# A late table, a shared opening and an earlier split: rearranging the start and the first group change of a gated linear attention and expert kernel

## The chip, the cores and the metric

The kernel runs on one core of a Trainium2 chip. The metric is the time of one execution on the device in microseconds (us). A core has five engines that each work through their own queue of instructions in order: TensorE (PE in the profile, PEld where it loads weights), VectorE (DVE), ScalarE (ACT), GpSimd (POOL) and SyncE (SP), which here only issues transfers. A queue's own instructions, such as the issue of a transfer, carry a q behind the engine's name (SPq, ACTq).

## The reference

Two blocks follow each other. The first is a gated linear recurrence over 768 time steps for 4 batches and 8 heads of 48 columns; the second is four experts of two layers each, weighted by normalised probabilities.

```python
for t in range(S):                      # B 4, H 8, S 768, D 48
    state = alpha[:, :, t, :, None] * state + einsum('bhd,bhe->bhde', k[:, :, t], v[:, :, t])
    y[:, :, t] = einsum('bhd,bhde->bhe', q[:, :, t], state)
x = y.transpose(0, 2, 1, 3).reshape(B * S, H * D)          # 3072 x 384
p = domain_probs / (domain_probs.sum(-1, keepdims=True) + 1e-09)
for e in range(4):                                          # w1 384 x 1024, w2 1024 x 384
    out += p[:, e:e + 1] * (np.maximum(x @ w1[e], 0.0) @ w2[e])
```

## The kernel before

**Units and groups.** A unit is 128 time steps of one batch; there are 24. A unit's attention yields 128 rows of x, transposed. Units are collected into groups: group 0 has two, groups 1 to 5 have four each, the last has two. A group is what the experts work on at a time.

**The attention of one unit** (`attention(u)`) is a generator. It loads nothing itself but asks for the raw inputs of a later unit as its own come free (`load(after, ...)`). It turns alpha, k and q on PE (`turned`, L270), copies alpha's and k's result out of PSUM on ScalarE (tile AT, L281; tile KT, L286), and multiplies q's by AT on VectorE (tile QT, L293). The terms of a row with itself are a product and a sum on VectorE (L289, L290, tile `dot`). Then come seven levels, each with twice the block width of the last: two ScalarE copies of a half of QT into a block tile (`copy_q`, L312), a product of QT with the decay (`next_q`, L319, and the decay's own product, L321), a ScalarE copy of a half of KT into the next KT tile (L330) and a VectorE product for the other half (L331, `next_k`). PE multiplies the blocks (`products`, L338; `far`, L393 for the last level), and VectorE puts the scores in their places under a mask (`take`, L348) in the tile `near`, which starts from the terms of a row with itself (L364). At the end ScalarE copies `far` (L406) and `near` (L410, twice, once for each half) into the tile `lat`, PE multiplies that with v (`yps`, L432), and ScalarE puts the result into the group's x (L448).

**The experts.** `up(gi, e, fc)` computes one of eight chunks of 128 hidden columns for a whole group; `down(gi, e, slots, between)` multiplies them with the second layer's weights for a unit and adds the sums up on VectorE or ScalarE (`add_up`). In group 0 the first layer works on plain float32 (L538). From group 1 on, x and the weights are split into parts with fewer bits each (`split_x`, `split_piece`), and L546 multiplies the parts: part 1 and 0 into the tile `one`, part 2 into `two`. Step 0 of `split_x` is three ScalarE copies (L502) that make part 0; each of the steps 1 to 3 makes the parts 1 and 2 of a third of x on VectorE (L252, L253). Split weights are written to DRAM from GpSimd's queue (`kept<-w`, L233) and read again by the later groups (L196).

**Order.** The program writes out the order of instructions itself; each engine takes them in that order. At the start, unit 0 runs alone with dummy matmuls (`fill`, L749) in between, so that PE stays busy; unit 1 follows behind, at first interleaved with it. From then on, `advance` adds up estimated costs of the expert work, and steps a unit's generator when its due time has come. Each step of `down` is one product of a unit with a chunk; `between` holds pieces of work to be put ahead of a given step. That is how the next group's x is split during the last second layer of the group before (expert 3). For group 0 that layer is called twice, once for each of its two units, with eight steps each.

**Loads.** The loads of the units and of the weights are issued from SP in the order of the program: `load(0, "akqv")`, `load(1, "akqv")`, and then the four pieces of the first expert's first layer (`load_piece(0, i)`, L214 and L215). The identity, the masks and the probabilities (`p_all`, 48 KB in runs of four floats) come from ScalarE's queue. `norm_probs` normalises the probabilities on VectorE after unit 0's attention (L257 to L261), and they are used when sums are added up.

Of the kernel before, what the change touches and what calls it, by code (L numbers as in the profile page):

```python
# [10 lines left out]
F32 = mybir.dt.float32  # L11
# [5 lines left out]
AX = mybir.AxisListType  # L17
# [3 lines left out]
def kernel(  # L21
# [37 lines left out]
    nc = tc.nc  # L59

    B, H, S, D = q.shape
    E, DM, F = moe_w1.shape
    P = 128
# [7 lines left out]
    NT = B * P  # L71
# [11 lines left out]
    n = np.arange(QUAD)[None, :]  # L83
# [7 lines left out]
    work = ctx.enter_context(tc.tile_pool(name="work", bufs=2))  # L91
# [7 lines left out]
    p_all = const.tile([P, NBLK, E], F32, name="p_all")  # L99
# [3 lines left out]
    near = const.tile([P, H, HALF], F32, name="near")  # L103
    lat = const.tile([P, H, P], F32, name="lat")
# [26 lines left out]
    def raw(u, nm):  # L131
        return values[u % 2] if nm == "v" else apart[nm] if u == 1 else early[nm]
# [27 lines left out]
    def load(u, names):  # L160
        if u >= len(units):
            return
        cb, b = units[u]
        for nm in names:
            src = srcs[nm][b, :, cb * P:(cb + 1) * P, :].rearrange("h s d -> s h d")
            if nm != "v":
                nc.sync.dma_start(out=raw(u, nm)[:, :, :D], in_=src)
                continue

            pairs = raw(u, nm).rearrange("p (a i) d -> p a i d", i=2)  # L170
            src = src.rearrange("p (a i) d -> p a i d", i=2)
            nc.sync.dma_start(out=pairs[:, :, 0, :D], in_=src[:, :, 0])
            nc.sync.dma_start(out=pairs[:, :, 1, :TAIL], in_=src[:, :, 1, QUAD:])
            nc.sync.dma_start(out=pairs[:, :, 1, TAIL:D], in_=src[:, :, 1, :QUAD])
# [13 lines left out]
    def load_piece(l, i, beside=False):  # L188
        if i >= E * NQ * LAST:
            return  # L190
        gi, k = divmod(i, E * NQ)
        e, c = divmod(k, NQ)
        if gi > l:
            w = wt[l][i] = wts.tile([P, 3, KC * QF], F32R, name=f"w{l + 1}",
                                    bufs=AHEAD if l == 0 else NQ)
            nc.sync.dma_start(out=w.bitcast(F32), in_=kept[l][k])  # L196
            return
        if l == 1 and not beside:
            return
        if l == 0:  # L200

            if gi > 0 or e == 0:
                shared[c] = wts.tile([P, 3, KC * QF], F32R, name="w2", bufs=NQ)
            w = shared[c][:, 2 - e % 2 if gi == 0 else 2].bitcast(F32)
        else:

            place = (hidden[c][:, 0] if not split2(gi, e, c) else hidden[c + NQ // 2][:, 1])
            w = place.rearrange("p f n -> p (f n)")[:, :KC * QF].bitcast(F32)
        wt[l][i] = w
        if l == 0:  # L210
            heads = moe_w1[e].rearrange("(h d) f -> h d f", d=D)[:, :, c * QF:(c + 1) * QF]
            w = w.rearrange("p (c f) -> p c f", f=QF)
            for part in range(2):
                nc.sync.dma_start(out=w[:, part], in_=heads[part * H // 2:(part + 1) * H // 2, :QUAD])  # L214
            nc.sync.dma_start(out=w[:, 2], in_=heads[:, QUAD:])  # L215
        else:
            nc.sync.dma_start(
                out=w.rearrange("p (c d) -> p c d", d=DM),
                in_=moe_w2[e].rearrange("(c p) d -> p c d", p=P)[:, c * FPQ:(c + 1) * FPQ])
# [44 lines left out]
    def halves(t, m):  # L264
        return t.rearrange("p a (b two r) -> p a b two r", two=2, r=m)

    def turned(src):
        tp = ps.tile([P, NP, P], F32, name="tp", tag="w")
        for p in range(NP):
            nc.tensor.transpose(tp[:, p, :], src(p), ident)  # L270
        return tp

    def attention(u):
        cb, b = units[u]
        ra, rk, rq, rv = (raw(u, nm) for nm in ("a", "k", "q", "v"))
# [6 lines left out]
        after = u + 2 if u == 0 else u + 1 if u > 1 else len(units)  # L282
# [1 line left out]
        yield  # L284
        KT = keys()
        nc.scalar.copy(out=KT, in_=turned(pair(rk)))  # L286
        own = work.tile([P, NT], F32, name="t")[:, :H * D].rearrange("p (h d) -> p h d", d=D)
        dot = work.tile([P, H], F32, name="dot")
        nc.vector.tensor_mul(own, rq[:, :, :D], rk[:, :, :D])  # L289
        nc.vector.reduce_sum(out=dot, in_=own, axis=AX.X)  # L290
        load(after, "k")
        yield
        nc.vector.tensor_mul(QT, turned(pair(rq)), AT)  # L293
        load(after, "q")
        yield

# [27 lines left out]
        def next_k(li):  # L324
            m = LEVELS[li]
            old = new = halves(KTs[li], m)
            if li + 1 < len(LEVELS):
                KTs.append(keys())
                new = halves(KTs[-1], m)
                nc.scalar.copy(out=new[:, :, :, 1, :], in_=old[:, :, :, 1, :])  # L330
            nc.vector.tensor_mul(new[:, :, :, 0, :], old[:, :, :, 0, :],  # L331
                                 spread(halved(decs[li])[:, :, :, 1], m))

# [70 lines left out]
        for s in range(2):  # L404
            rows = slice(HALF * s, HALF * (s + 1))
            nc.scalar.copy(out=parts[:HALF, :, s, :, HALF:], in_=far[rows])  # L406
        yield
        for s in range(2):
            rows = slice(HALF * s, HALF * (s + 1))
            nc.scalar.copy(out=lat[rows, :, rows], in_=near[rows])  # L410
        KT = KTs[-1]
        yield

# [49 lines left out]
        if cb < NCB - 1:  # L463
# [5 lines left out]
            for i in range(2):  # L469
                rows = slice(HD * i, HD * (i + 1))  # L470
                old, add = st[rows, :, i, :], sps[rows, :, i, :]
# [251 lines left out]
    with tc.manual_schedule():  # L723
        nc.scalar.dma_start(out=ident_all, in_=nc.inline_tensor(ident_np, name="ident_c").ap())
        nc.scalar.dma_start(out=masks, in_=nc.inline_tensor(mask_np, name="masks_c").ap())
        nc.scalar.dma_start(out=p_all, in_=moe_domain_probs.rearrange("(n p) e -> p n e", p=P))
        nc.gpsimd.memset(sts[B - 1], 0.0)
        for nm in "akq":
            for r in (early[nm], apart[nm]):
                nc.gpsimd.memset(r[:, :, D:], 0.0)  # L730
        nc.gpsimd.memset(lat[HALF:, :, :HALF], 0.0)
        for t in values + blocks:
            nc.gpsimd.memset(t, 0.0)
        for t in sts[:-1]:
            nc.gpsimd.memset(t, 0.0)

        load(0, "akqv")
        load(1, "akqv")
        for i in range(NQ):
            load_piece(0, i)  # L740

        idle = ps.tile([P, P], F32, name="idle", tag="g", bufs=4)
        zeros = sts[B - 1].rearrange("p a i d -> p (a i d)")[:, :P]

        def fill(n):
            for _ in range(n):
                nc.tensor.matmul(idle, lhsT=zeros, rhs=zeros, start=True, stop=True)  # L749

        runs = [attention(u) for u in range(len(groups[0]))]
        fill(8)
        for u, n in ((0, 3), (0, 6), (0, 4), (0, 5), (0, 5), (0, 4), (0, 3), (1, 0), (0, 0), (0, 2),
                     (0, 2), (1, 2), (0, 2), (1, 0), (0, 0), (0, 4), (0, 4), (0, 0)):
            next(runs[u])
            fill(n)
        norm_probs()

        span = cost(0, 0, 0) * FCH / 2 + cost(1, 0, 0)
        waiting.extend((span * (k + 1) / 15, u, runs[u])  # L760
                       for k, u in enumerate([1, 1, 1, 0, 1, 0, *[1] * 8]))
        for fc in range(FCH):
            up(0, 0, fc, slice(0, 1))
            advance(cost(0, 0, 0) / 2)
        down(0, 0, [0], deque())
        while waiting:
            next(waiting.popleft()[2], None)
        clock = 0.0
        waiting.extend((1.0 + k, 1, runs[1]) for k in range(2))
        waiting.extend(deal())  # L770

        for (gi, e), after in zip(tasks, [*tasks[1:], (None, None)]):
            rest = gi == e == 0
            for fc in range(FCH):
                up(gi, e, fc, slice(1, len(groups[0])) if rest else None)
                advance(cost(0, gi, e) / (2 if rest else 1))
            each = len(groups[gi]) if split2(gi, e) else 1
            turns = [range(k, k + each) for k in range(rest, len(groups[gi]), each)]
            for k, slots in enumerate(turns):

                between = deque()
                if after[1] == 0:
                    for step, at in enumerate((0.0, 0.6, 0.7, 0.78)):
                        at = at * len(turns) - k
                        if 0 <= at < 1:
                            between.append((at, lambda step=step: split_x(after[0], step)))
                down(gi, e, slots, between)
        while stores:
            stores.popleft()()
# [28 lines left out]
```

## The time and the profile before

| What | Value |
|---|---|
| Time, median of 3 runs | 1064.21 us (1062.67 to 1064.66) |
| Span of the profiled execution | 1062.8 us |
| Mean granted clock of PE | 0.998 |
| PE busy | 1041.9 us, 98% |
| VectorE busy | 781.6 us, 74% |
| ScalarE busy | 569.0 us, 54% |
| GpSimd busy | 32.9 us, 3% |
| First matmul of the first layer starts | 26.22 us |
| First matmul of group 1's first layer starts | 165.66 us |

Busy time is the time in which an engine worked on an instruction, and a share of it is an average over all stages: it tells which engine can be the limit, not where. A line of the timeline gives the start in microseconds from the span's start, the duration, the engine, the source line, the operation, the tiles written and read, and how many like instructions follow each other; in brackets stands how long the engine was idle before it, and what it then waited for. A line of the waits gives the engine and the line that waited, what it waited for, the total in microseconds, how often, and the longest.

### The profile page before, as it was taken

Reading aid. Unit: us, or ns where it says so; the run is one execution under the profiler, and the core shown is the slowest. Engines: PE = TensorE matmul, PEld = TensorE weight load, DVE = VectorE, ACT = ScalarE, POOL = GpSimd, SP = SyncE. Lnnn points to the kernel's source line nnn. Section 1 sums busy time; section 2 is a strip of 40 time slices with the busy share of each in tenths; the row PEclk is TensorE's granted clock in tenths of the full one; section 3 lists DMA queues with packets and bytes.
Section 4 is the critical chain, followed back from the end, with each engine's and each line's share of the span. In section 5 each row is a group of like instructions: output and inputs, shape, how many; then the busy total and the mean of one; then the engine's idle time right before and its main releaser. Section 6 shows DMA issues by size and latency. Waiting matters only on the chain.

```text
span 1062.8 us, 21599 instructions
## 1 busy us (share of the span) xinstructions
PE 1041.9 (98%) x8508; PEld 906.2 (85%) x8508; DVE 781.6 (74%) x1619; ACT 569.0 (54%) x1202; POOL 32.9 (3%) x71
## 2 busy tenths in 40 slices
PE   8899999999999999999999999999999999999998
PEld 7777776687788898898898998988989889898988
DVE  5488777677779877778877877986877875666565
ACT  5687875665756555536546435555464443323232
POOL 2010010000001000000000000000000000000000
PEclk9999999999999999999999999999999999999999
DMA  8596799797977957758669559586594454444531
GB/s 124 157 325 202 245 318 352 272 339 241 307 256 271 376 180 276 279 165 315 249 187 364 201 190 339 172 307 231 167 373 174 194 208 170 187 179 178 197 160 45
DMA packets 158838, 251.66 MB, mean 237 GB/s; under 512 B 120113, under 2 KB 135345, under 8 KB 136209
## 3 DMA queue, kind: packets, MB, share of 16 engines
q1 hardware_dynamic: 149600, 208.82, 57.3%
q0 software_dynamic: 5760, 41.29, 9.7%
q8 instruction: 67, 1.10, 0.4%
q10 hardware_dynamic: 3376, 0.17, 0.3%
q14 instruction: 35, 0.28, 0.1%
HBM read 207.79 MB, written 42.47 MB: 235 GB/s over the span
## 4 chain that ended last, share of the span: by engine, by line
PE 85%; ACT 5%; DVE 5%; DMA 2%; issue 2%; SPq 1%; ACTq 0%; DVEq 0%
PE ops L639 36%; PE one L546 23%; PE two L546 11%; PE sc L338 6%; PE yps L432 3%; PE tp L270 3%; ACT qb L312 2%; PE one L538 1%; PE sps L467 1%; PE far L393 1%; DMA hT<-in_moe_w_dram 1%; DVE w L230 1%; ACT KT L330 1%; DMA rq<-in_q_dram 1%; SPq L214 1%
## 5 line engine op out<-in xcount | busy, mean ns | idle before, releaser
L639 PE MATMUL ops<-w,hT 128*128 128x384 f32 x1872 | 347.4, 340 | 0.2 <-DVE hT L592 0.2
L639 PEld LDWEIGHTS ops<-w,hT 128*128 128x128 f32 x1872 | 325.4, 188 | 4.7 <-ACT t L557 0.6
L546 PE MATMUL one<-xT,w 128*128 128x512 f32 x960 | 254.4, 400 | 2.7 <-DVE xT L252 2.3
L546 PEld LDWEIGHTS one<-xT,w 128*128 128x128 f32 x960 | 176.3, 189 | 42.2 <-DVE xT L252 4.0
L557 ACT ACTIVATE t<-one 128x512 f32<-128x512 f32 (+1 forms) x192 | 107.2, 558 | 180.7 <-PE one L546 175.3
L312 ACT COPY qb<-QT 64x256 f32<-64x256 f32 x336 | 136.6, 407 | 71.2 <-DVE QT L293 42.7
L586 DVE SCALAR_TENSOR_TENSOR hT<-t,hT 128x512 fp32r<-128x512 f32 (+1 forms) x172 | 110.5, 643 | 68.3 <-ACT hT L584 65.8
L559 DVE TENSOR_TENSOR t<-t,two 128x512 f32<-128x512 f32 (+1 forms) x172 | 109.5, 636 | 58.0 <-ACT t L557 29.3
L584 ACT ACTIVATE hT<-t 128x512 fp32r<-128x512 f32 (+1 forms) x172 | 101.8, 592 | 86.4 <-DVE t L559 85.3
L546 PE MATMUL two<-xT,w 128*128 128x512 f32 x480 | 136.9, 394 | 0.0
L546 PEld LDWEIGHTS two<-xT,w 128*128 128x128 f32 x480 | 90.6, 189 | 20.2 <-DVE acc L668 0.2
L639 PE MATMUL ops<-hT 128*128 128x384 f32 x288 | 100.9, 491 | 0.3 <-DMA hT<-in_moe_w_dram 0.3
L592 DVE SCALAR_TENSOR_TENSOR hT<-hT 128x512 fp32r<-128x512 f32 (+1 forms) x172 | 101.0, 634 | 0.0
L348 DVE COPY_PREDICATED near<-masks,sc 128x256 f32<-128x256 uint8 x144 | 76.9, 534 | 19.2 <-PE sc L338 16.3
L319 DVE TENSOR_TENSOR QT<-QT,dec 128x256 f32<-128x256 f32 x144 | 60.8, 423 | 36.0 <-ACT qb L312 35.3
L338 PEld LDWEIGHTS sc<-qb,KT 128*64 128x64 f32 x2304 | 72.7, 138 | 9.3 <-issue 4.7
L338 PE MATMUL sc<-qb,KT 128*64 128x64 f32 x2304 | 77.2, 223 | 2.6 <-ACT qb L312 2.6
L639 PEld LDWEIGHTS ops<-hT 128*128 128x128 f32 x288 | 52.1, 190 | 29.6 <-DMA hT<-in_moe_w_dram 0.9
L668 DVE SCALAR_TENSOR_TENSOR acc<-ops,p_all,acc 128x384 f32<-128x384 f32 x82 | 49.9, 615 | 30.4 <-PE ops L639 29.2
L330 ACT COPY KT<-KT 128x256 f32<-128x256 f32 x144 | 60.0, 417 | 3.1
L331 DVE TENSOR_TENSOR KT<-KT,dec 128x256 f32<-128x256 f32 x144 | 60.2, 418 | 0.0
L538 PE MATMUL one<-xT,w 128*128 128x256 f32 (+1 forms) x240 | 46.2, 340 | 0.6 <-ACT xT L448 0.6
(88 smaller groups left out, 934.2 us busy)
## 6 DMA issues: line engine op xcount, KB each, us to landing
w<-kept SPq DMA_DIRECT2D x144, 1152.0 KB
kept<-w POOLq DMA_DIRECT2D x32, 1152.0 KB, 7.9
hT<-in_moe_w_dram SPq DMA_DIRECT2D x32, 384.0 KB
w<-in_moe_w_dram SPq DMA_DIRECT2D x48, 128.0 KB
ra<-in_alpha_dram SPq DMA_DIRECT2D x23, 192.0 KB
rk<-in_k_dram SPq DMA_DIRECT2D x23, 192.0 KB
rq<-in_q_dram SPq DMA_DIRECT2D x23, 192.0 KB
out_dram<-acc POOLq DMA_DIRECT2D x18, 192.0 KB, 7.9
```

What stands on the lines that cost most here:

```text
L312: nc.scalar.copy(out=qb[rows, :, i, :].rearrange("p a (b r) -> p a b r", r=m), in_=qv[rows])
L319: nc.vector.tensor_mul(qv, qv, spread(dv[:, :, :, 0], m))
L330: nc.scalar.copy(out=new[:, :, :, 1, :], in_=old[:, :, :, 1, :])
L338: nc.tensor.matmul(out[HALF * s:HALF * (s + 1), 2 * p:2 * p + 2, :], lhsT=KTs[li][:, p, HALF * s:HALF * (s + 1)], rhs=qbs[li][:, p, :, QUA ...
L348: nc.vector.copy_predicated(near.rearrange("p a (b two r) -> p a b two r", two=2, r=m)[:, :, :, 1, :], mk.unsqueeze(1).broadcast_to([P, H, ...
L546: nc.tensor.matmul(out, lhsT=w[:, part, kc], rhs=x_part(gi, part, kc), start=(part == terms[0] and kc == 0), stop=(part == terms[-1] and k ...
L557: nc.scalar.activation(out=t, in_=one, func=ACT.Copy, scale=FINE)
L559: nc.vector.tensor_add(t, t, two)
L584: nc.scalar.activation(out=top, in_=x, func=ACT.Relu, scale=TRIM)
L586: nc.vector.scalar_tensor_tensor(out=low, in0=x, scalar=0.0, in1=top.bitcast(F32), op0=ALU.max, op1=ALU.subtract)
L592: nc.vector.scalar_tensor_tensor(out=dif, in0=top.bitcast(F32), scalar=1 / 4096.0, in1=low.bitcast(F32), op0=ALU.mult, op1=ALU.subtract)
L639: nc.tensor.matmul(sums[at], lhsT=h, rhs=w, start=(n == begins[at]), stop=(n == ends[at]))
```

## The change

The change has three parts.

The load of the probabilities goes from ScalarE's queue, where it was issued among the first inputs, to SP's queue behind the inputs of the first two units and ahead of the first weights. It is for the first inputs to have the DMA engines to themselves.

In unit 0, which runs with nothing else beside it, the work of the attention is spread over four engines. The terms of a row with itself are computed after QT and not before. The copies of KT's half (six of them) go from ScalarE to GpSimd, and the second copy of `near` into `lat` goes to VectorE. The number of dummy matmuls goes from 8 to 7 at the start, from 3 to 2 after the first step and from 6 to 3 after the second.

For group 1 alone, steps 1 to 3 of `split_x` are placed at 0.30, 0.42 and 0.54 of group 0's last second layer instead of 0.60, 0.70 and 0.78. It is for x to be ready when PE arrives at group 1.

```diff
-        nc.vector.tensor_mul(own, rq[:, :, :D], rk[:, :, :D])
-        nc.vector.reduce_sum(out=dot, in_=own, axis=AX.X)
-        load(after, "k")
+        def own_terms():
+            own = work.tile([P, NT], F32, name="t")[:, :H * D].rearrange("p (h d) -> p h d", d=D)
+            nc.vector.tensor_mul(own, rq[:, :, :D], rk[:, :, :D])
+            nc.vector.reduce_sum(out=dot, in_=own, axis=AX.X)
+            load(after, "k")
+        alone = u == 0
+        if not alone:
+            own_terms()
         yield
         nc.vector.tensor_mul(QT, turned(pair(rq)), AT)
+        if alone:
+            own_terms()
...
-                nc.scalar.copy(out=new[:, :, :, 1, :], in_=old[:, :, :, 1, :])
+                copy = nc.gpsimd.tensor_copy if alone else nc.scalar.copy
+                copy(out=new[:, :, :, 1, :], in_=old[:, :, :, 1, :])
...
-            nc.scalar.copy(out=lat[rows, :, rows], in_=near[rows])
+            copy = nc.vector.tensor_copy if alone and s else nc.scalar.copy
+            copy(out=lat[rows, :, rows], in_=near[rows])
...
-        nc.scalar.dma_start(out=p_all, in_=moe_domain_probs.rearrange("(n p) e -> p n e", p=P))
...
         load(1, "akqv")
+        nc.sync.dma_start(out=p_all, in_=moe_domain_probs.rearrange("(n p) e -> p n e", p=P))
         for i in range(NQ):
             load_piece(0, i)
...
-        fill(8)
-        for u, n in ((0, 3), (0, 6), (0, 4), (0, 5), (0, 5), (0, 4), (0, 3), (1, 0), (0, 0), (0, 2),
+        fill(7)
+        for u, n in ((0, 2), (0, 3), (0, 4), (0, 5), (0, 5), (0, 4), (0, 3), (1, 0), (0, 0), (0, 2),
...
-                    for step, at in enumerate((0.0, 0.6, 0.7, 0.78)):
+                    for step, at in enumerate((0.0, 0.3, 0.42, 0.54) if gi == 0 else
+                                              (0.0, 0.6, 0.7, 0.78)):
```

More of the change, by code (lines that the diff above doesn't have):

```diff
@@ L286, in attention @@
         nc.scalar.copy(out=KT, in_=turned(pair(rk)))
-        own = work.tile([P, NT], F32, name="t")[:, :H * D].rearrange("p (h d) -> p h d", d=D)
         dot = work.tile([P, H], F32, name="dot")
-        nc.vector.tensor_mul(own, rq[:, :, :D], rk[:, :, :D])
-        nc.vector.reduce_sum(out=dot, in_=own, axis=AX.X)
-        load(after, "k")
+        def own_terms():
[6 more added lines that the diff above has]
+            own_terms()
         yield
         nc.vector.tensor_mul(QT, turned(pair(rq)), AT)
+        if alone:
+            own_terms()
         load(after, "q")
```

## The prediction

> **What bounds the kernel now.** I read the page first, then the waits of PE, then the timeline of the two places where PE waits and that the change touches, then windows of one microsecond over the second of them.
>
> From the page, busy time by engine and the chain that ended last:
>
> ```profile
> PE 1041.9 (98%) x8508; PEld 906.2 (85%) x8508; DVE 781.6 (74%) x1619; ACT 569.0 (54%) x1202; POOL 32.9 (3%) x71
> PE 85%; ACT 5%; DVE 5%; DMA 2%; issue 2%; SPq 1%; ACTq 0%; DVEq 0%
> ```
>
> PE is the bound almost everywhere. It can be sped up only where it waits, where its clock is low, or where it does no useful work. The waits of PE, longest first:
>
> ```profile
> PE yps L432 <- ACT lat L410: 3.1, 4, 1.5
> PE far L393 <- ACT qb L312: 3.0, 2, 1.6
> PE sc L338 <- ACT qb L312: 2.6, 3, 1.2
> PE one L546 <- DVE xT L252: 2.3, 4, 0.8
> ```
>
> The first two belong mostly to the opening[...]; the fourth is the group change. The timeline of the opening (start, duration, engine, line):
>
> ```profile
> 1.65 0.59 ACTq L726 DMA_DIRECT2D p_all<-in_moe_domain_probs_dram  x1
> 1.86 0.96 SPq L167 DMA_DIRECT2D rq<-in_q_dram  x1
> 8.61 0.56 DVE L289 TENSOR_TENSOR t<-rq,rk 128x384 f32<-128x384 f32 x1 [8.61 <-DMA rq<-in_q_dram]
> 8.65 0.63 PE L270 MATMUL tp<-ident,rq 128*128 128x128 f32 x4 [0.72 <-DMA rq<-in_q_dram]
> 9.68 0.68 DVE L293 TENSOR_TENSOR QT<-tp,AT 128x512 f32<-128x512 f32 x1
> 10.45 0.87 ACT L312 COPY qb<-QT 64x256 f32<-64x256 f32 x2 [3.25 <-DVE QT L293]
> 11.34 0.45 ACT L330 COPY KT<-KT 128x256 f32<-128x256 f32 x1
> 11.35 0.43 DVE L319 TENSOR_TENSOR QT<-QT,AT 128x256 f32<-128x256 f32 x1 [0.99 <-ACT qb L312]
> 11.87 0.86 ACT L312 COPY qb<-QT 64x256 f32<-64x256 f32 x2
> 23.24 1.24 ACT L410 COPY lat<-near 64x512 f32<-64x512 f32 x2 [1.14 <-DVE near L348]
> 26.22 3.62 PE L538 MATMUL one<-xT,w 128*128 128x128 f32 x30 [0.60 <-ACT xT L448]
> ```
>
> The chain hangs on q, the third load: it lands at 8.6 us, 6.7 us after its issue began, and everything up to the first useful matmul at 26.22 follows from it. The probabilities were issued just before it and are first read at 23.4 us.
>
> The timeline at the group change:
>
> ```profile
> 165.66 0.50 PE L546 MATMUL one<-xT,w 128*128 128x512 f32 x1 [0.17 <-DVE xT L252]
> 166.99 0.50 PE L546 MATMUL one<-xT,w 128*128 128x512 f32 x1 [0.83 <-DVE xT L252]
> 168.32 2.08 PE L546 MATMUL one<-xT,w 128*128 128x512 f32 x4 [0.83 <-DVE xT L252]
> ```
>
> And the same place in windows (width, then busy PE, PEld, DVE, ACT, POOL, then PE clock, DMA share, GB/s):
>
> ```profile
> 169.00:170.00 1.00, 1.00 (x4) 0.81 (x3) 1.00 (x4) 0.00 (x0) 0.00 (x0) 0.50 1.02 426
> 170.00:171.00 1.00, 1.00 (x3) 0.77 (x3) 0.27 (x1) 0.56 (x1) 0.43 (x1) 0.50 0.99 419
> ```
>
> PE waits three times for VectorE to split x, and the short starvation drops its clock to half from about 168.4 to 171.4. The dip costs as much as the waits.
>
> [...]
>
> **The change part by part.**
>
> *p_all behind the first inputs.* In the first 60 us the ACT queue's 3,376 packets take 4.6% of 16 engines, 2.76 us of every engine. 48 KB in runs of 16 bytes are 3,072 of these, so by packets p_all is 2.5 us of each engine. If all of it stood ahead of q, q lands at 8.56 - 2.5 = 6.1. The other bound: k lands at 5.9 as before and q takes its 192 KB at the 160 GB/s of windows 10 to 13, thus 7.1. I take 6.5. Transposes of q also stand behind PE's fills: k's transposes at about 5.6 take 0.6, three fills are six instructions of 0.115, so 6.9. The smaller counts of fills (7, 2, 3 for 8, 3, 6) are what makes that possible: they remove 1.2 to 1.4 us of dummies. So the transposes of q run 6.9 to 7.5 instead of 8.65 to 9.28.
>
> *own_terms after QT.* L289 and L290 took VectorE from 8.61 to 9.7, though QT's input was there at 9.3. That is 0.35 us; the 1.1 us now fall into the 0.99 us that VectorE waits for the first copy of q, 0.1 over. QT starts at 7.6 instead of 9.68: 2.1 us.
>
> *KT copies to GpSimd.* Per level the path is two qb copies (0.87), one QT product (0.43) and handovers (0.08), 1.38; ScalarE with its KT copy takes 1.42. So this gives 0.04 on two levels and some 0.3 on levels 3 to 5, where ScalarE also copies for unit 1; from 15 us on VectorE is full and takes most of that back. [...] New KT halves are wanted a level later (2 us), so duration itself is hidden. I count the edit at nothing, +1.0 to -0.4.
>
> *Second lat copy to VectorE.* Two copies of 0.62 in line become one beside one. VectorE is busy to 23.52 (KT of level 6), then copies 0.4 to 0.6: ready at 24.0 instead of 24.48, 0.4 us. norm_probs, queued behind, has its first reader at 46.9 us (the first sum, L666).
>
> First useful matmul: 26.22 - 2.1 - 0.4 = about 23.8. Then comes the risk. The first-layer weights stream from about 14 us at 109 GB/s (mean of windows 14 to 24), four pieces of 393 KB: 14.4 us, so the fourth lands at 28.4, and as p_all now stands ahead of them on the same queue, not sooner. The seventh chunk wanted it at 30.75 (4.5 us after the first `one`) and will at 28.3. I take off 0.4 us, half of the 0.1 to 0.7 that p_all's tail may add: 2.1 us remain. After that issues, loads and copies are triggered by shifted instructions and PE keeps the lead; between 46 and 165 us its waits are for ScalarE, which shift along.
>
> *The split.* len(turns) is 2, so steps 1 to 3 moved from steps 2, 4 and 5 of the second block's eight to 5 and 7 of the first block's and 1 of the second's. No instruction is added. PE took from 165.49 to 171.2 for the first chunk's nine matmuls; chunks a little later take 2.06 (starts 181.96 and 184.02). So 3.6 us can be had. VectorE has idle 0.55 before 156.77 and 0.77 before 159.93; three splits of 1.41 moved ahead end, adding up its queue, at 165.5: near, split, level 3 and two masked copies to 160.1, split to 161.5, sum to 162.1, weight split to 164.05, split to 165.5. That is just when PE asks. Queued behind: L289, L290, level 4, two masked copies, level 5, and the sum L668 that frees a PSUM bank, done at about 169.7 where PE wants it at 169.4. I take off 0.3: 3.3 us. Also the last weight split ends 1.65 us later, and with it the store to kept (10 us to land) and the load behind it, which I put at 179.3; PE wants that piece about 180.5.
>
> **Sum:** 1064.2 - 2.1 - 3.3 = 1058.8, rounded to 1059.0.
>
> **The rivals.**
> A. The start gains nothing lasting (weights of the first layer arrive at the old time, or GpSimd's copies hold VectorE): for it the weights' slow stream, against it their slack of a few microseconds on pieces 1 to 3. Only 3.3 us: 1060.9.
> B. The split gains little since the late weight piece, or VectorE's backlog, becomes the new wait: for it VectorE is full from 157 to 169 and DMA at 420 GB/s; against it, the slack of 1.2 us. Start 2.1 plus 1: 1061.1; with none of it, 1062.1.
> C. Slower: [...] p_all delays the weights by its whole 2.5 us, and a new gap near 170 halves the clock once more (3 us at half, 1.5): 6.4 us lost against 5.4 gained, 1065.2. Nothing in the trace shows these together.
>
> **How the numbers follow.** Forecast (both gains, 4 to 6.5 us) 0.67; A 0.15; B 0.13, of which 0.04 with no split gain at all; C 0.05. The best case is 2.9 + 3.7, 1057.6, and single runs differ by 1 us either way, so I go to 1056.8 below; 1062.2 above takes in A and B. Faster by over 0.2% means below 1062.1: 0.87; same 0.09, from B's end and half-cancelled gains; slower 0.04.
>
> **What would show it.** q's wait on VectorE ends at 6.5 to 7; QT starts near 7.6; [...] the first `one` matmul is near 23.9; the wait of PE `one` for xT is gone and the clock stays at 1.00 near 165; the distance from that first `one` to the first L546 matmul stays 139.4 us. It is wrong if q lands after 7.5, if products stretch beside GpSimd, or if PE waits for w near 28 or 180.

## The result: 1057.99 us, and where the time came from

| | Before | After |
|---|---|---|
| Median | 1063.84 us (4 runs) | 1057.99 us (4 runs, 1057.43 to 1059.19) |
| Ratio, 95% interval | | 0.9947 (0.9930 to 0.9965) |
| First matmul of the first layer | 26.22 us | 24.16 us |
| First matmul of group 1's first layer | 165.66 us | 163.70 us |

A second set of runs gave the changed kernel a ratio of 0.9962 (0.9948 to 0.9975). The gain is 4.0 to 5.6 us; the intervals are 1.9 us (first set) and 1.4 us (second) to either side. One of the five runs of the second set took 1280.98 us at a mean granted clock of 0.753 and is left out of the ratio.

The page after, busy time by engine (in its words PE busy, PEld busy and so on):

```profile
PE 1039.5 (98%) x8498; PEld 905.3 (86%) x8498; DVE 782.1 (74%) x1620; ACT 565.4 (53%) x1195; POOL 35.5 (3%) x77
```

The work is the same, but for ten matmuls that are no longer there (five dummies of two instructions each) and the copies that moved. Of the 5.4 us by which the profiled span is shorter, 2.4 us are busy time of PE (fewer dummies, and a clock of 1.00 where it was 0.50), the rest is waiting. The waits of PE after, longest first, with some left out:

```profile
PE yps L443 <- ACT lat L421: 2.8, 3, 1.5
PE sc L348 <- ACT qb L321: 2.6, 3, 1.2
...
PE one L557 <- DMA w<-kept: 1.2, 1, 1.2
PE one L549 <- DMA w<-in_moe_w_dram: 0.8, 1, 0.8
...
PE one L557 <- DVE xT L252: 0.5, 1, 0.5
```

The wait for xT went from 2.3 to 0.5 us; what is left is one wait at 344 us, at the change to group 2, whose split wasn't moved. Two waits for transfers are new, and they stand where the work in front of them has become faster: 0.8 us for the first layer's weights and 1.2 us for the first split weights read back.

The timeline of the opening after (lines chosen):

```profile
6.97 0.63 PE L270 MATMUL tp<-ident,rq 128*128 128x128 f32 x4
7.71 0.69 DVE L300 TENSOR_TENSOR QT<-tp,AT 128x512 f32<-128x512 f32 x1 [7.71 <-PE tp L270]
8.32 0.55 DVE L291 TENSOR_TENSOR t<-rq,rk 128x384 f32<-128x384 f32 x1
8.49 0.87 ACT L321 COPY qb<-QT 64x256 f32<-64x256 f32 x2 [1.46 <-DVE QT L300]
10.35 0.56 SPq L749 DMA_DIRECT2D p_all<-in_moe_domain_probs_dram  x1
21.50 0.62 ACT L421 COPY lat<-near 64x512 f32<-64x512 f32 x1 [1.14 <-DVE near L358]
21.81 0.42 DVE L421 COPY lat<-near 64x512 f32<-64x512 f32 x1
22.49 1.08 PE L443 MATMUL yps<-lat,rv 128*32 128x128 f32 x32
24.16 3.62 PE L549 MATMUL one<-xT,w 128*128 128x128 f32 x30 [0.59 <-ACT xT L459]
29.89 1.10 PE L549 MATMUL one<-xT,w 128*128 128x128 f32 x4 [0.79 <-DMA w<-in_moe_w_dram]
```

The transposes of q start 1.7 us sooner and without a wait for q; QT starts 2.0 us sooner, the first useful matmul 2.06.

At the group change, the end of the first chunk before (its beginning stands in the prediction):

```profile
170.20 1.48 PE L546 MATMUL two<-xT,w 128*128 128x512 f32 x3
```

Timeline and windows (width, busy PE, PEld, DVE, ACT, POOL, clock, DMA share, GB/s) after:

```profile
163.70 1.63 PE L557 MATMUL one<-xT,w 128*128 128x512 f32 x6 [1.20 <-DMA w<-kept]
165.17 0.86 PE L557 MATMUL two<-xT,w 128*128 128x512 f32 x3
```

```profile
169.00:170.00 1.00, 1.00 (x6) 0.79 (x6) 0.74 (x3) 0.96 (x3) 0.00 (x0) 1.00 0.95 395
170.00:171.00 1.00, 1.00 (x6) 0.84 (x5) 0.91 (x3) 0.98 (x4) 0.00 (x0) 1.00 0.54 208
```

The nine matmuls of the first chunk now run in one piece, at a clock of 1.00, within 2.3 us of their start instead of 6.0.

A ruler for all that follows: PE's last-level product `far` (L393 before) occurs once in each of the 24 units. Its starts in two profiles, subtracted, show where time is gained. Us ahead of the profile of before:

| `far` before at | after | again | split only | loads and dummies only | chain only | no GpSimd copies |
|---|---|---|---|---|---|---|
| 20.65 | 1.73 | 1.22 | -0.11 | 1.39 | -0.30 | 1.88 |
| 40.45 | 2.50 | 2.04 | -0.09 | 1.42 | 0.51 | 2.01 |
| 131.34 | 2.49 | 2.08 | -0.04 | 1.44 | 0.55 | 2.03 |
| 178.27 | 5.68 | 5.48 | 4.61 | 1.33 | 2.24 | 5.23 |
| 845.12 | 5.65 | 5.47 | 4.73 | 1.66 | 2.54 | 5.70 |

What the change does is decided in two places, before 40 us and between 131 and 178 us. From 40 to 131 us and from 178 to 845 us no column moves by more than 0.5. Behind 845 us, where the change touches nothing, the profiles still differ: to the end of the span they gain a further -0.2 (after) to +1.2 us (loads and dummies only) on the profile of before. So the time of a single run says less about the change than the ruler does, and the ruler itself compares single profiles.

### The profile page after: what moved, and what is told of

The parts are those of the page before. It is cut to its first block, busy times and chain, and to the rows that moved or that the text cites. A ratio compares the mean times of both kernels' runs of the same rounds, so it can differ in the third digit from the quotient of the medians.

```text
span 1057.4 us, 21578 instructions
## 1 busy us (share of the span) xinstructions
PE 1039.5 (98%) x8498; PEld 905.3 (86%) x8498; DVE 782.1 (74%) x1620; ACT 565.4 (53%) x1195; POOL 35.5 (3%) x77
## 4 chain that ended last, share of the span: by engine, by line
PE 83%; ACT 4%; DVE 4%; SPq 4%; DMA 3%; issue 2%; POOL 0%; ACTq 0%; DVEq 0%; POOLq 0%
PE ops L650 35%; PE one L557 23%; PE two L557 11%; PE sc L348 5%; PE yps L443 3%; PE tp L270 3%; SPq L214 2%; ACT qb L321 1%; PE one L549 1%; PE sps L478 1%; DMA w<-kept 1%; PE far L403 1%; SPq L215 1%; DMA w<-in_moe_w_dram 1%; DVE w L230 1%
## 5 line engine op out<-in xcount | busy, mean ns | idle before, releaser
L340 ACT COPY KT<-KT 128x256 f32<-128x256 f32 x138 | 57.5, 417 | 3.0
```

## The experiments

**Theory:** the start gains since q lands sooner, with the dummies cut to fit; the group change gains by the waits for xT and the clock, less a new wait for the weights read back. **Rivals:** the spread over four engines makes the start; VectorE's backlog sets the group change; what is gained in front is lost in the transfers behind. Times are medians; ratios are to the kernel before on the same chip.

### One part at a time

Split alone:

```diff
-                    for step, at in enumerate((0.0, 0.6, 0.7, 0.78)):
+                    for step, at in enumerate((0.0, 0.3, 0.42, 0.54) if gi == 0 else
+                                              (0.0, 0.6, 0.7, 0.78)):
```

> The kernel before with only the three split steps moved. My theory: the waits for xT and the half clock go (3.6 us to be had), but PE then waits about 1.2 us for the first piece of split weights read back from kept, so 2.4 to 2.7 us remain: ratio 0.9975, PE clock 1.00 near 165 us, the first split matmul right after a wait for DMA w<-kept. Rival (VectorE's backlog eats it): no wait for DMA w<-kept, but waits of PE for VectorE's sums or for t near 168 to 172 us, and under 1.5 us gained.

Measured: 1059.61 us, ratio 0.9975 (0.9966 to 0.9984), thus 2.7 us. The waits of PE between 155 and 175 us in its profile are one line:

```profile
PE one L546 <- DMA w<-kept: 0.5, 1, 0.5
```

No wait for VectorE is left there, so the backlog isn't the limit. The ruler shows 4.65 us between 131 and 178, more than the 3.6 that I thought were to be had. Part of it is in two waits of before in this stretch (at 142 and 154 us) that this profile lacks:

```profile
PE yps L432 <- DVE QT L293: 0.6, 1, 0.6
PE ops L639 <- DMA hT<-in_moe_w_dram: 0.3, 1, 0.3
```

Both come ahead of group 1, and nothing shows that the split removed them; the first is back in the changed kernel (0.5).

Loads and dummies alone:

```diff
-        nc.scalar.dma_start(out=p_all, in_=moe_domain_probs.rearrange("(n p) e -> p n e", p=P))
         load(1, "akqv")
+        nc.sync.dma_start(out=p_all, in_=moe_domain_probs.rearrange("(n p) e -> p n e", p=P))
...
-        fill(8)
-        for u, n in ((0, 3), (0, 6), (0, 4), (0, 5), (0, 5), (0, 4), (0, 3), (1, 0), (0, 0), (0, 2),
+        fill(7)
+        for u, n in ((0, 2), (0, 3), (0, 4), (0, 5), (0, 5), (0, 4), (0, 3), (1, 0), (0, 0), (0, 2),
```

> The kernel before with only p_all behind the first inputs and the smaller counts of dummy matmuls; terms of a row with itself before QT, all copies on ScalarE. My theory: q lands between 6.2 and 6.9 us, which VectorE's wait for it shows; the transposes of q run at about 7.0 and QT starts at about 7.9, first useful matmul near 24.5 instead of 26.22, 2 us gained in all, ratio 0.998. Rival (the spread over four engines makes the gain at the start): QT not before 9 us and under 0.7 us gained.

Measured: 1062.24 us, ratio 0.9993 (0.9985 to 1.0001). VectorE's wait for q, in its profile:

```profile
DVE t L289 <- DMA rq<-in_q_dram: 7.1, 1, 7.1
```

q lands at 7.1 us, against 8.6, later than the 6.2 to 6.9 that I expected. The dummies run on PE, and the load of q is issued before 2 us and waits for nothing there, so it is the place of p_all that moved q. QT starts at 8.27 and the first useful matmul at 24.83: 1.4 us gained where 1.7 were expected, and the ruler keeps 1.44 as far as 131 us. In the time 0.7 us show, of which the interval can't tell 0 from 1.6.

The chain alone (terms of a row with itself after QT, KT copies on GpSimd, second near copy on VectorE), the other edits undone, with these lines of the change:

```diff
+        if alone:
+            own_terms()
...
+                copy = nc.gpsimd.tensor_copy if alone else nc.scalar.copy
+                copy(out=new[:, :, :, 1, :], in_=old[:, :, :, 1, :])
...
+            copy = nc.vector.tensor_copy if alone and s else nc.scalar.copy
+            copy(out=lat[rows, :, rows], in_=near[rows])
```

> The kernel before with only unit 0's chain changed: terms of a row with itself after QT, KT copies on GpSimd, second near copy on VectorE; p_all, dummy matmuls and split as before. My theory: q still lands at 8.6, QT starts at 9.35 (0.35 sooner), the end gains 0.25 to 0.35 more, first useful matmul near 25.6, 0.6 us gained: ratio 0.9994, not told from 1 in the time. Rival: first useful matmul before 24.8 and 1.5 us or more gained.

Measured: 1061.94 us, ratio 0.9993 (0.9985 to 1.0001). q landed 0.33 us later than in the profile of before; from the start of its transposes to QT it takes 0.74 us instead of 1.03, so the edit gains 0.29. The first useful matmul came at 26.19. From the start of q's transposes to there it takes 17.21 us instead of 17.57: 0.36 in all, where 0.6 were expected. This alone doesn't make the start.

Its profile showed something else. The windows at the group change:

```profile
168.00:169.00 1.00, 1.00 (x6) 0.83 (x5) 1.00 (x5) 0.20 (x1) 0.00 (x0) 1.00 1.03 433
169.00:170.00 1.00, 1.00 (x8) 0.81 (x8) 0.97 (x2) 0.40 (x1) 0.18 (x1) 1.00 1.02 433
```

and the timeline there:

```profile
166.25 0.50 PE L557 MATMUL one<-xT,w 128*128 128x512 f32 x1 [0.82 <-DVE xT L252]
167.57 1.19 PE L557 MATMUL one<-xT,w 128*128 128x512 f32 x4 [0.83 <-DVE xT L252]
168.60 0.86 PE L557 MATMUL two<-xT,w 128*128 128x512 f32 x3
```

The three waits for xT are as in the kernel before, but the clock stayed at 1.00. That is nearly all of the 1.69 us which the ruler shows for this kernel between 131 and 178: the fall of the clock doesn't follow from the waits in every execution. No run here shows what else decides it.

How often the clock falls can be read from all runs, since each lists its mean granted clock. The four profiles with a fall at a wait (before, loads and dummies alone, and the two kernels below that delay a weight piece) have a mean of 0.998, the other ten 0.999 or 1.000. A mean of 0.998 or less came in 41 of the 91 runs of the kernel before that stand beside the experiments, in 8 of 13 with the loads and dummies alone, in 6 of 13 with the chain alone, and in none of the 43 runs of the kernels that have the earlier split and whose weight pieces aren't delayed. Sorted by it, mean times in us (runs), all on one chip:

| | With the fall | Without it |
|---|---|---|
| Before | 1063.5 (15) | 1061.9 (15) |
| Split alone | | 1059.6 (10) |
| Loads and dummies alone | 1062.4 (8) | 1061.0 (5) |
| Chain alone | 1062.8 (6) | 1061.2 (7) |

The fall costs the kernel before 1.6 us here, and 1.0 to 1.3 on the three other chips. Like compared with like, the split gains 2.3 us (give or take 0.4, a 95% interval of the means), the loads and dummies 1.1 (0.4), the chain 0.7 (0.4); the split also ends the falls. This sorting was made after the runs and is no part of what was expected.

KT copies back on ScalarE:

```diff
-                copy = nc.gpsimd.tensor_copy if alone else nc.scalar.copy
+                copy = nc.scalar.copy
```

> The changed kernel with the six KT copies of unit 0 back on ScalarE. My theory (the copies were hidden on ScalarE as well, and those on GpSimd stretch one or two VectorE products by 0.1 to 0.2): first useful matmul within 0.3 us of 24.16, the time within 0.1%. Rival (moving them is what frees the chain): first useful matmul at 25 or later, 0.8 us or more lost.

Measured: 1058.30 us, ratio 0.9962 (0.9950 to 0.9975); the changed kernel has 0.9962 and 0.9947. First useful matmul at 24.02. Moving the copies gains nothing. The timelines show why it rather costs: VectorE in the changed kernel, and GpSimd beside it,

```profile
13.07 0.69 DVE L374 TENSOR_TENSOR near<-ident,dot 128x512 f32<-128x512 f32 x1
13.29 0.73 POOL L340 COPY KT<-KT 128x256 f32<-128x256 f32 x1 [0.90 <-DVE KT L341]
13.68 0.62 DVE L328 TENSOR_TENSOR QT<-QT,dec 128x256 f32<-128x256 f32 x1
14.89 0.40 POOL L340 COPY KT<-KT 128x256 f32<-128x256 f32 x1 [0.87 <-PE sc L348]
```

and VectorE with the copies on ScalarE:

```profile
13.06 0.68 DVE L374 TENSOR_TENSOR near<-ident,dot 128x512 f32<-128x512 f32 x1
13.66 0.42 DVE L328 TENSOR_TENSOR QT<-QT,dec 128x256 f32<-128x256 f32 x1
```

A copy on GpSimd took 0.40 or 0.41, and 0.73 where VectorE's product for `near` (0.69) was under way; the product that started in this copy took 0.62 instead of 0.42. Another (at 10.81 us, with 0.23 us of a copy left) took 0.51 instead of 0.43. A third started 0.13 us before the end of a copy and wasn't longer (0.43). So three of six copies overlap a product, and two of them cost VectorE 0.3 us in all. In the three delays (0.33, 0.20 and 0.08 us) the later instruction lost 0.14 to 0.15 us less than what was left of the earlier one by its recorded end (0.47, 0.34 and 0.23).

### The start: dummies and the order of loads

Old counts of dummies in the changed kernel:

```diff
-        fill(7)
-        for u, n in ((0, 2), (0, 3), (0, 4), (0, 5), (0, 5), (0, 4), (0, 3), (1, 0), (0, 0), (0, 2),
+        fill(8)
+        for u, n in ((0, 3), (0, 6), (0, 4), (0, 5), (0, 5), (0, 4), (0, 3), (1, 0), (0, 0), (0, 2),
```

> The changed kernel with the old counts of dummy matmuls, 8, 3 and 6. Theory: the dummies stand ahead of q's transposes, which start 0.7 to 1.0 us later than with 7, 2 and 3 (at 7.8 to 8.1 us), and the first useful matmul is at 24.8 to 25.3: without the smaller counts the earlier q would be half lost. Rival: the transposes wait for q anyway, and the start is as in the changed kernel.

Measured: 1058.89 us, ratio 0.9959 (0.9945 to 0.9973). The transposes of q started at 7.87 us, QT at 8.58, the first useful matmul at 25.03: the 0.9 us of the expectation are there, and at 131 us the kernel is 1.68 us ahead instead of 2.49. The time doesn't show it: at 178 us this profile (of the fastest of the five runs, 1056.88 us) is 6.14 us ahead, more than that of the changed kernel. What the stretch from 131 to 178 adds differs from run to run by as much as such an edit is worth.

Fewer dummies still (one ahead of q's transposes, two ahead of the last products):

```diff
-        for u, n in ((0, 2), (0, 3), (0, 4), (0, 5), (0, 5), (0, 4), (0, 3), (1, 0), (0, 0), (0, 2),
-                     (0, 2), (1, 2), (0, 2), (1, 0), (0, 0), (0, 4), (0, 4), (0, 0)):
+        for u, n in ((0, 2), (0, 1), (0, 4), (0, 5), (0, 5), (0, 4), (0, 3), (1, 0), (0, 0), (0, 2),
+                     (0, 2), (1, 2), (0, 2), (1, 0), (0, 0), (0, 4), (0, 2), (0, 0)):
```

> The changed kernel with one dummy matmul instead of three ahead of q's transposes, and two instead of four ahead of unit 0's last products. Theory: the dummies hold up q's transposes (no wait for the q load is left ahead of them) and the last products (they start 0.26 us after lat is ready); without them QT starts 0.2 to 0.45 us sooner and the first useful matmul is at 23.5 to 23.8 instead of 24.16. Rival: PE's clock falls for want of work, or q has only just landed, and the first useful matmul stays at 24.1 or later.

Measured: 1057.65 us, ratio 0.9955 (0.9943 to 0.9968). The first part held: PE then waits for q, 0.34 us, and the transposes start at 6.85. The second part fell. The last products still start 0.26 us after the copy's end (22.11 to 22.37), now as a wait for VectorE:

```profile
22.37 1.08 PE L443 MATMUL yps<-lat,rv 128*32 128x128 f32 x32 [0.44 <-DVE lat L421]
```

It wasn't the dummies; 0.26 lie between the recorded end of the VectorE copy and the start of its reader, as in the profile after (22.23 to 22.49). Behind the ScalarE copy of before, which ended at 24.48, it was 0.06:

```profile
24.54 1.08 PE L432 MATMUL yps<-lat,rv 128*32 128x128 f32 x32 [0.32 <-ACT lat L410]
```

Probabilities loaded behind the first four weight pieces:

```diff
-        nc.sync.dma_start(out=p_all, in_=moe_domain_probs.rearrange("(n p) e -> p n e", p=P))
         for i in range(NQ):
             load_piece(0, i)
+        nc.sync.dma_start(out=p_all, in_=moe_domain_probs.rearrange("(n p) e -> p n e", p=P))
...
-        norm_probs()
...
-        down(0, 0, [0], deque())
+        down(0, 0, [0], deque([(0.7, norm_probs)]))
```

> The changed kernel with the probabilities loaded behind the first four weight pieces and normalised late in the first second layer. Theory: the weight stream starts about 2 us sooner, the wait of PE for DMA w<-in_moe_w (0.8 and 1.2 us in the two profiles that have the whole start) is gone; of that the third unit of time gained stays only in part, as unit 1's chain on ScalarE and VectorE sets the pace until 45 us: 0 to 0.5 us at the next landmarks. Rival: the wait sets the pace, and all of 0.8 to 1.2 us is gained.

Measured: 1057.87 us, ratio 0.9960 (0.9946 to 0.9973). The wait for DMA w<-in_moe_w is gone, and of the 0.8 us nothing is left at 40 us (2.54 ahead, 2.50 in the changed kernel): unit 1's chain on ScalarE sets the pace there, as expected.

### The group change: what the new wait is

The changed kernel again, with no edit:

> The changed kernel once more, on one chip with the next three, as their measure. Theory: ratio 0.9947 to 0.996 to the kernel before; at group 1's first split matmul a wait for DMA w<-kept between 0 and 1.3 us, as in the runs so far (1.20, 0.49, 0.64, 0). Rival (the wait of 1.2 was the profile's chance): none at all in this one, and the ratio at 0.994.

Measured: 1058.31 us, ratio 0.9962 (0.9948 to 0.9975), with a wait of 0.17 us for DMA w<-kept. So the wait is real, but 1.2 us is the longest in any profile. With the split alone it was 0.5, and 0.3 with the old counts of dummies. In the last kernel below, the profile puts a wait of 0.70 us of this matmul down to VectorE's QT, a tile that it doesn't read. It started there 0.35 us after the store to `kept` issued beside the load had landed, as it did after (0.31), here (0.30) and with the split alone (0.30), so I count it as the same wait.

The first piece alone on its queue:

```diff
                     load_piece(0, i + 1 + k)
+                    if k == 0:
+                        nc.sync.dma_start(out=gate, in_=wt[0][i + 1][:1, 0, :16].bitcast(F32))
```

> The changed kernel with a 64-byte transfer on SyncE's queue that reads the first split weight piece, put between the loads of the first and the second piece: the second can't start before the first has landed. Theory A (the first piece shares the DMA engines with the second piece's load): it lands 2 us or more sooner, PE's wait for DMA w<-kept is gone, up to 1.2 us gained. Theory B (it shares them with the stores to kept alone): the wait stays, and the second piece's later landing may add one at the third chunk.

Measured: 1061.40 us, ratio 0.9992 (0.9983 to 1.0001). SyncE's queue:

```profile
153.64 0.61 SPq L197 DMA_DIRECT2D w<-kept  x1
163.88 0.26 SPq L587 DMA_DIRECT2D gate<-w  x1
```

The transfer behind the first piece could start at 163.88: the piece had taken 10.2 us though no second load was under way. From its issue to the start of the first split matmul, which waited for it, it took 11.3 and 10.4 us in the changed kernel's two profiles, so the second load can have held it up by 0.2 to 1.1 us, not by the 2 or more of theory A, which falls. The second piece, so delayed, cost a wait of 2.5 us at the third chunk, and the clock fell to half behind it, from about 172.7 us.

```profile
171.27 1.70 PE L558 MATMUL one<-xT,w 128*128 128x512 f32 x6 [2.46 <-DMA w<-kept]
```

A store held back until the first piece has landed, on GpSimd's queue:

```diff
-        nc.gpsimd.dma_start(out=kept[l][i % (E * NQ)], in_=w.bitcast(F32))
+        store = lambda: nc.gpsimd.dma_start(out=kept[l][i % (E * NQ)], in_=w.bitcast(F32))
+        if (l, i) == (0, E * NQ - 2):
+            held.append(store)
+        else:
+            store()
...
                     load_piece(0, i + 1 + k)
+                    if k == 0:
+                        nc.gpsimd.dma_start(out=gate, in_=wt[0][i + 1][:1, 0, :16].bitcast(F32))
+                        held.pop()()
```

> The changed kernel with the store of split weight piece 14 held on GpSimd's queue until the first piece of group 1 has been read back. Theory B of the last experiment (that load shares the DMA engines with the stores to kept): it lands 2 us or more sooner, PE never waits for DMA w<-kept at the first split matmul, and the range of the times narrows; 0 to 1.2 us gained. Rival: it lands as before, as the DMA engines are full with other transfers.

Measured: 1061.31 us, ratio 0.9980 (0.9972 to 0.9988). GpSimd's queue:

```profile
162.32 0.50 POOL L592 DMA_DIRECT2D gate<-w  x1 [10.40 <-DVE w L234]
162.86 0.56 POOL L235 DMA_DIRECT2D kept<-w  x1
```

The piece, issued at 153.97, had landed by 162.32, in 8.3 us instead of 10.2, and the first split matmul (163.42) follows the work ahead of it without a wait for it. But the store went out 10 us later and landed 5 us later (at 168.66 us, instead of 163.39 in the profile after), and the third load, which is issued right behind this landing in both, went out at 168.81 instead of 163.53. PE waited for the third piece:

```profile
176.76 1.62 PE L563 MATMUL one<-xT,w 128*128 128x512 f32 x3 [2.66 <-DMA w<-kept]
```

The clock fell behind this wait too (0.58 from 176 to 177 us, 0.50 to 179). Theory B was right in its direction and worth 2 us of landing, and useless: from 143 to 172 us the DMA engines are full (share 1.05 before, 1.02 after, 395 and 392 GB/s), and in both of these experiments what one transfer gained another lost.

Dummies in the waits of the kernel before:

```diff
                         nc.tensor.matmul(out, lhsT=w[:, part, kc], rhs=x_part(gi, part, kc),
                                          start=(part == terms[0] and kc == 0),
                                          stop=(part == terms[-1] and kc == KC - 1))
+                        for _ in range(3 if gi == 1 and e == fc == 0 and part == 1 and kc < 2 else 0):
+                            nc.tensor.matmul(two, lhsT=w[:, 0, 0], rhs=x_part(gi, 0, 0),
+                                             start=True, stop=True)
```

> The kernel before with three dummy matmuls (overwritten later) in each of the first two waits for xT, 0.7 us of work in 0.83 us of waiting. Theory: the waits stay but the clock doesn't fall, nine matmuls end 1.65 us sooner than with a clock of one half; as the fall doesn't come in every execution, 0.5 to 1.6 us gained in the median and the slowest runs vanish: ratio 0.9985 to 0.9995. Rival (the clock falls for another cause than idle PE): clock 0.50 near 168 us all the same.

Measured: 1062.90 us, ratio 0.9993 (0.9985 to 1.0001). The clock stayed at 1.00 and the nine matmuls took 3.8 us with the dummies between. In this profile the first of them waited for the weights read back, as in the profile of the loads and dummies alone:

```profile
166.33 0.47 PE L546 MATMUL one<-xT,w 128*128 128x512 f32 x1 [0.88 <-DMA w<-kept]
```

As the fall was missing in the chain-only profile without any dummies, one profile with a full clock doesn't prove that they held it. The mean clocks say more: 0.998 or less in one of the 13 runs with the dummies, and in 14 of the 35 of before on the same chip. If the dummies did nothing, a difference this large would come by chance about once in 33 times, so this speaks for them without settling it. The median time agrees with the expectation, and with no change.

### All that looked useful

KT copies on ScalarE, fewer dummies and probabilities behind the weights, in one kernel:

> The changed kernel with what the runs speak for: KT copies back on ScalarE, fewer dummy matmuls ahead of q's transposes and of the last products, probabilities loaded behind the first four weight pieces. Theory: each of them adds a little at the start (0.2, 0.3, and the wait for the fourth weight piece), the first useful matmul is near 23.5, the landmark at 131 us 2.6 to 3.0 us ahead of the kernel before; the full DMA engines between 143 and 172 us take part of it back: ratio 0.9945 to 0.996. Rival (what is gained at the start is always lost at 164 us): ratio 0.996 or more, as for the changed kernel.

Measured: 1057.48 us, ratio 0.9951 (0.9937 to 0.9964). It is the lowest median, 0.5 us under the changed kernel's, and not told from it: the changed kernel had 0.9947 and 0.9962. The first useful matmul came at 24.08, not 23.5, since q landed at 7.1 us and the last products kept their 0.26 us.

## Why the prediction was right

Forecast 1059.0 (1056.8 to 1062.2), measured 1057.99; direction and size hold.

- **p_all and q.** Forecast: q at 6.5 (6.1 to 7.1). Measured where an engine waited for it: 7.1 alone and in the last kernel, 6.85 with fewer dummies. In the profile after it was there by 6.97, in the second one by 7.4, where the transposes stood behind dummies. With p_all moved, q landed 1.5 us sooner (7.1, against 8.6), as the prediction has it; the landing lies in the late half of the range. Without the cut of the dummies 0.9 us of it would be lost, as the old counts show.
- **own_terms.** Forecast 0.35 us, measured 0.29.
- **KT copies.** Counted at nothing, and worth nothing (0.9962 with the copies on ScalarE, 0.9962 and 0.9947 with them on GpSimd). In two of six copies VectorE's product lost time beside GpSimd, 0.08 and 0.20 us, and in one the copy did, 0.33: what was left of the other one, less some 0.15 us. The copies took 0.40 or 0.41 us, and 0.73 once. Of the 6.4 us lost in rival C, 2.5 and 1.5 were for p_all and the clock; the rest was put on GpSimd's copies as a guess, since no profile of before had one beside VectorE.
- **Second lat copy.** Forecast 0.4, measured 0.31 (1.30 from its start to the last products before, 0.99 after): the copy is shorter, the handover behind it longer.
- **First useful matmul.** Forecast 23.8, measured 24.16 and 24.67. Of 2.4 us there are 2.06 and 1.55.
- **Weights of the first layer.** I had taken off 0.4 us for their late landing. The wait is there (0.79 us at 29.9), but it cost nothing at 40 us, where the lead is 2.50, and 2.54 in the kernel that has no such wait: PE then waits for unit 1's chain on ScalarE.
- **The split.** Forecast 3.3 us. Measured 2.7 (1.7 to 3.6) in time, alone; in the ruler 3.2 and 3.4 beside the start, 4.65 alone. The 3.6 to be had rest on a misreading: what follows the nine matmuls of before starts at 171.48 us, not 171.2, so 3.9 were to be had in that profile. I had the right danger and the wrong piece: I let the fourth weight piece be late at 180 us, and it was the first at 163, in a wait that xT had hidden before. VectorE's backlog, the other half of rival B, isn't seen: the last step of the split ends at 162.00 us, half a microsecond before PE is through with what stands ahead of group 1.
- **The clock.** I counted 1.65 us of the 3.6 as a fall that comes each time. The chain-only profile shows the same waits without it, and by the mean clocks it came in 41 of 91 runs of before, at 1.0 to 1.6 us each. PE had waited 1.8 us in three pieces, none above 0.83. The windows of before (0.59, 0.50, 0.50 and 0.70 from 168 to 172 us) make 3.4 us at half clock.
- **The distance** from the first `one` to the first split matmul was to stay 139.4 us; it is 139.5. That is chance: the ruler gained 0.4 us on the way and 0.5 more before 163, and the new wait of 1.2 us took the rest.

Two of the signs of being wrong that I had named came true, a product that stretched beside GpSimd (0.62 us) and a wait of PE for w near 30 us (0.79); neither undid the gain.

By the ratios, 0.25, 0.07 and 0.07% alone make 0.39%, the whole 0.38 and 0.53%. Sorted by the clock, the parts make 2.3 + 1.1 + 0.7 = 4.1 us without a fall. The second set of the changed kernel gains 3.5 us (give or take 1.2) on the runs of before without one, and the three kernels that differ from it by one edit at the start, KT copies on ScalarE, fewer dummies or late probabilities, gain 3.7 to 4.2. So the parts add up within the noise. The falls that are gone, in 45% of the runs of before, add about 0.6 us on the average (my estimate, from 1.3 us each).

The direction and the parts of the sum were right; that it came so close is partly luck. The start brought 1.8 us in time instead of 2.1. The split was credited with too much, a fall of the clock in every run and no wait at 163 us, and with too little, as the 3.6 was 0.3 too low and the 0.3 for VectorE's backlog wasn't needed. Rival A, that the start gains nothing lasting, is rejected at the landmarks (2.0 to 2.5 us ahead at 131 us) and in the sorted times; how much of it passes through the stretch with full DMA engines stays open. Unsorted, the time speaks for 0.7 us with the start's loads and dummies alone, and for 1.4 or 3.0 us with all of the start beside the split (0.9975 to 0.9962 or 0.9947).

## What to carry to other kernels

A small transfer can be a long one: 48 KB in 16-byte runs stood in the way of an input that the first step waits for, and with it moved behind what is needed first, by one line, that input landed at 7.1 us instead of 8.6. The queue that it left had 3,376 packets and 4.6% of the 16 DMA engines' time in the first 60 us before, and 288 and 1.0% after, which makes some 2.2 us less on each engine (an estimate from these two). When a wait is removed, look at once for what else the waiting instruction needs, and where the transfer engines are full (a DMA share of 1.05 and 1.02 here), don't move one transfer ahead without asking which one it pushes back. An edit that frees an engine which the path doesn't wait for gained nothing here (0.9962 with the KT copies on ScalarE); compare the alternation of the path (here copy, product, copy) with the engine's own load before moving work. Where an event such as a fall of the clock comes in some runs only, find a number that every run records, and sort the runs by it before comparing.

## What the runs showed of the hardware

- PE's clock fell to 0.50 after 1.8 to 1.9 us of waiting spread over 2.8 us, in the profile of before (three waits for xT, of 0.17, 0.83 and 0.83) and in that of loads and dummies alone (one for the weights, two for xT; three lines of its timeline and a window):

```profile
164.73 0.47 PE L546 MATMUL one<-xT,w 128*128 128x512 f32 x1 [0.64 <-DMA w<-kept]
165.59 0.51 PE L546 MATMUL one<-xT,w 128*128 128x512 f32 x1 [0.40 <-DVE xT L252]
166.92 2.04 PE L546 MATMUL one<-xT,w 128*128 128x512 f32 x4 [0.82 <-DVE xT L252]
167.00:168.00 1.00, 1.00 (x3) 0.81 (x4) 1.00 (x4) 0.00 (x0) 0.00 (x0) 0.50 1.04 442
```

- With the waits of before it stayed at 1.00 in the chain-only profile. It also fell after single waits of 2.46 us (first piece alone) and 2.66 us (store held back). Each of the four falls lasted 3.4 us.
- In the profile after, a GpSimd copy of 128x256 float32 took 0.40 or 0.41 us, and 0.73 when it began 0.47 us before the end of a VectorE product of 128x512; a product that began 0.34 us before the end of a copy took 0.62 instead of 0.42, one that began 0.23 us before it 0.51 instead of 0.43, and one that began 0.13 us before it was not longer (0.43).
- In the profile after, a VectorE copy of 64x512 float32 was recorded with 0.42 us, and PE started on its result 0.26 us later, as with fewer dummies; behind ScalarE's copy of the same size (0.62) in the profile of before it started 0.06 later.
- One load of 1,152 KB took 10.2 us to land beside the stores (first piece alone), with the DMA engines at 360 GB/s (mean from 153 to 164 us), and 8.3 with one store less (store held back).
